# Fourier mixing and a gated convolution layer on one core: two matrix products per step in place of three, with work moved to ScalarE, VectorE and GpSimd

## Chip, cores and metric

The kernel runs on one core of one Trainium2 chip. The time is the device time in microseconds of one execution. A ratio is the mean time of one kernel's runs over that of the kernel before in the same rounds on the same chip, so it is not quite the ratio of the medians that are quoted beside it. "Faster" and "slower" mean by over 2%.

## The reference

```python
# x: (8, 3136, 256); w_in (256, 1024); conv_w (3, 1024); w_out (1024, 256), all float32
X = np.fft.fft(np.fft.fft(x, axis=1), axis=2).real      # mixing block
h = np.maximum(X @ w_in, 0.0)
conv_out = sum over k of conv_w[k] * (h shifted by k - 1 rows, zeros outside)
gate = 1.0 / (1.0 + np.exp(-conv_out))
out = (h * gate) @ w_out
```

## The kernel before

The mixing block is folded into `P` (cosines, even in the output row k) and `Q` (sines, odd in k; its last feature, the cosine feature D/2, is even). So columns k of `P` and `Q` give the rows k and S-k. The first layer works in **steps**: one batch, one chunk of columns (four per batch: 385, 386, 386 and 418 columns), one group of 128 features (eight per chunk); 256 steps in all, and 32 per batch. A step adds `G0 P + G1 Q` in a PSUM bank, takes the Relu (rows k), adds `G2 Q` with `G2 = -2 G1` in the same bank, and takes the Relu again (rows S-k, backwards). The rows of `h` are 769 to 833 columns wide. The second layer runs three steps behind.

```python
def front(s):                       # (cut)
    for i in range(2):
        mm(xs[s][:, 0:n], G[:, i, fs], PQ[b][i][:, ch.k0:ch.k1], i == 0, i == 1)
    act(h[:, ch.front], xs[s][:, 0:n], AF.Relu)

def back(s):                        # (cut)
    mm(xs[s][:, 0:n], G[:, 2, fs], PQ[b][1][:, ch.k0:ch.k1], False, True)
    act(hs[s][:, ch.back][:, ::-1], xs.pop(s)[:, ch.cols], AF.Relu)

def conv(s):                        # all three on VectorE
    ts(out=g, in0=h[:, 0:n], scalar1=cw[:, 0, f:f + 1], scalar2=None, op0=ALU.mult)
    for k in (1, 2):
        stt(out=g, in0=h[:, k:k + n], scalar=cw[:, k, f:f + 1], in1=g, op0=ALU.mult, op1=ALU.add)

def gate(s):
    act(g, g, AF.Sigmoid)
    vt(g, g, hs.pop(s)[:, 1:g.shape[1] + 1], op=ALU.mult)      # VectorE

# the order, step si; late: the second layer of step si - 3
front(si); late[:half]; back(si); late[half:]; conv(si); gate(si - 1); side work
```

Side work is the next batch's folds (VectorE, twelve operations per batch), its four DFT stages (16 matrix products each, then a copy on ScalarE and two sums on VectorE), and two such stages for the D/2 feature per pair of batches.

## Time and profile before

| | before |
|---|---|
| time, median of the first 3 runs | 1536.83 us (1535.79 to 1539.03) |
| TensorE busy | 1452.7 us, 95% |
| VectorE, ScalarE, GpSimd busy | 1143.9, 536.5, 68.5 us |
| an ordinary step, from the chain of waits | 4.53 us, TensorE without a gap |

The page has the busy time of each engine, its busy tenths in forty slices, the chain of work that ended last, and groups of instructions (line, engine, operation, output and inputs, shapes, count; then total busy us and mean ns; then the engine's idle time just before them and who ended it). The lines are in the prediction.

### The profile page before, as it was taken

The page shows a single profiled execution, that of the slowest core. Times are in us where ns is not written, and L with a number is a line of the kernel's source. Part 1 is how long each engine was busy: PE and PEld are TensorE (multiplying, and loading weights), DVE is VectorE, ACT ScalarE, POOL GpSimd, SP SyncE. Part 2 cuts the span into 40 slices and gives each one's busy share as a digit, 9 for nine tenths or more (in the row PEclk, how much of TensorE's full clock was granted, in tenths as well). Part 3 has the DMA queues.
Part 4 walks back from the last instruction along what each step waited for, and adds up shares of the span by engine and source line. Part 5 has one row for each costly group of instructions (what it writes and reads, how often), then busy time and mean ns, then how long its engine had stood idle before and what let it go on. Part 6 is the DMA issues. An engine that isn't in the chain of part 4 may idle for free.

```text
span 1535.6 us, 14574 instructions
## 1 busy us (share of the span) xinstructions
PE 1452.7 (95%) x5434; PEld 1003.6 (65%) x5434; DVE 1143.9 (74%) x1540; ACT 536.5 (35%) x1019; POOL 68.5 (4%) x81
## 2 busy tenths in 40 slices
PE   1758899999999999999999999999999999999998
PEld 0225556777767756677767756677766667677776
DVE  7699966689668966589767976679866666667775
ACT  0103323344334432344333433334423334334443
POOL 1201200001000100001000100000000000000000
PEclk9979999999999999999999999999999999999999
DMA  8501420013000220002200220000000000000001
GB/s 259 160 0 43 105 63 0 21 40 81 28 21 23 63 60 4 21 23 64 63 21 7 68 53 21 21 23 21 21 1 21 23 21 22 21 0 23 24 28 33
DMA packets 39014, 62.09 MB, mean 40 GB/s; under 512 B 5604, under 2 KB 30844, under 8 KB 38292
## 3 DMA queue, kind: packets, MB, share of 16 engines
q1 hardware_dynamic: 29084, 32.36, 6.4%
q0 software_dynamic: 8352, 24.21, 6.1%
q10 hardware_dynamic: 1508, 4.61, 1.0%
q8 instruction: 42, 0.69, 0.2%
q14 instruction: 28, 0.23, 0.1%
HBM read 35.41 MB, written 25.69 MB: 40 GB/s over the span
## 4 chain that ended last, share of the span: by engine, by line
PE 84%; DVE 10%; DMA 2%; ACT 2%; issue 1%; SPq 0%; ACTq 0%; DVEq 0%
PE pb L76 44%; PE po L76 41%; DMA out_dram<-os 2%; DVE g L364 2%; DVE xh L131 1%; DVE xh L124 1%; DVE g L369 1%; ACT os L388 1%; ACT g L368 1%; DVE g L362 1%; DMA raw<-in_moe_w_in_dram 1%; DVE w L141 0%; DVE nt L278 0%; DVE nt L266 0%; DVE nt L279 0%
## 5 line engine op out<-in xcount | busy, mean ns | idle before, releaser
L76 PE MATMUL po<-wout,g 128*128 128x256 f32 (+2 forms) x3200 | 773.4, 379 | 6.9 <-DVE g L369 6.7
L76 PEld LDWEIGHTS po<-wout,g 128*128 128x128 f32 (+2 forms) x3200 | 597.9, 187 | 216.2 <-issue 41.9
L364 DVE SCALAR_TENSOR_TENSOR g<-h,cw,g 128x770 f32<-128x770 f32 (+2 forms) x512 | 531.5, 1038 | 18.1
L76 PE MATMUL pb<-qt,G 128*128 128x386 f32 (+2 forms) x1024 | 426.4, 498 | 24.6 <-ACT h L346 17.2
L362 DVE TENSOR_SCALAR g<-h,cw 128x770 f32<-128x770 f32 (+2 forms) x256 | 161.3, 630 | 238.1 <-ACT h L354 233.3
L346 ACT ACTIVATE h<-pb 128x386 f32<-128x386 f32 (+2 forms) x256 | 127.9, 500 | 418.3 <-PE pb L76 393.3
L76 PEld LDWEIGHTS pb<-qt,G 128*128 128x128 f32 x1024 | 193.4, 190 | 118.8 <-ACT h L346 24.9
L369 DVE TENSOR_TENSOR g<-g,h 128x770 f32<-128x770 f32 (+2 forms) x256 | 248.8, 972 | 14.2 <-ACT g L368 14.2
L354 ACT ACTIVATE h<-pb 128x386 f32<-128x386 f32 (+2 forms) x256 | 127.9, 500 | 334.6 <-PE pb L76 334.6
L368 ACT ACTIVATE g<-g 128x770 f32<-128x770 f32 (+2 forms) x256 | 218.8, 855 | 22.8 <-DVE g L364 22.5
L76 PE MATMUL pb<-pt,G 128*128 128x386 f32 (+2 forms) x512 | 213.6, 499 | 3.0 <-DVE pt L174 3.0
L76 PE MATMUL pb<-tab,w 98*128 98x393 f32 (+7 forms) x512 | 173.7, 492 | 0.0
L76 PEld LDWEIGHTS pb<-tab,w 98*128 98x128 f32 (+3 forms) x512 | 96.5, 189 | 66.7 <-issue 0.7
L76 PEld LDWEIGHTS pb<-pt,G 128*128 128x128 f32 x512 | 97.0, 191 | 31.9 <-issue 5.9
L388 ACT COPY os<-po 128x256 f32<-128x256 f32 (+2 forms) x200 | 65.1, 375 | 53.0 <-DMA out_dram<-os 31.9
L76 PE MATMUL pb<-tab,ea 98*2 98x393 f32 (+7 forms) x160 | 56.3, 504 | 8.0 <-DVE ea L144 8.0
L171 ACT COPY as<-pb 128x393 f32<-128x393 f32 (+7 forms) x42 | 20.4, 485 | 120.3 <-PE pb L76 120.3
L76 PE MATMUL pb<-win,dm 128*128 128x512 f32 x24 | 15.7, 812 | 36.0 <-DVE nt L271 20.9
L93 POOL DMA_DIRECT2D xh<-in_x_dram x14 | 10.5, 752 | 822.6 <-DVE h L343 619.4
L76 PEld LDWEIGHTS pb<-tab,ea 98*2 98x2 f32 (+3 forms) x160 | 12.7, 85 | 47.7 <-issue 38.2
L98 POOL DMA_INDIRECT xh<-in_x_dram,idx x32 | 42.3, 1321 | 10.0 <-issue 9.7
L124 DVE TENSOR_TENSOR xh<-xh 99x1020 f32<-99x1020 f32 (+1 forms) x32 | 38.8, 1214 | 0.0
(46 smaller groups left out, 246.1 us busy)
## 6 DMA issues: line engine op xcount, KB each, us to landing
out_dram<-os SPq DMA_DIRECT2D x184, 128.0 KB
xh<-in_x_dram POOLq DMA_DIRECT2D x14, 784.0 KB, 6.6
tab<-dft_seq_dram SPq DMA_DIRECT2D x4, 1215.8 KB
raw<-in_moe_w_in_dram ACTq DMA_DIRECT2D x2, 1024.0 KB
raw<-in_moe_w_out_dram ACTq DMA_DIRECT2D x1, 2048.0 KB
xh<-in_x_dram SPq DMA_DIRECT2D x2, 784.0 KB
out_dram<-os SPq DMA_DIRECT2D x8, 127.0 KB
out_dram<-os SPq DMA_DIRECT2D x8, 65.0 KB
```

The costliest lines, as they stand in the source:

```text
L76: nc.tensor.matmul(o, l, r, start=start, stop=stop, skip_group_check=True)
L98: nc.gpsimd.indirect_dma_start(out=t[0:NP, 2 + s].rearrange("p q d -> p (q d)"), out_offset=None, in_=bass.AP(tensor=x.tensor, offset=x.of ...
L124: vt(a[:, :, 1:D], a[:, :, 1:D], r[:, :, D - 1:0:-1], op=ALU.add)
L131: vt(t[k, 3 - par], t[k, 0], t[k, 1], op=ALU.subtract if par else ALU.add)
L171: nc.scalar.copy(out=a, in_=ps[0])
L346: act(h[:, ch.front], xs[s][:, 0:n], AF.Relu)
L354: act(hs[s][:, ch.back][:, ::-1], xs.pop(s)[:, ch.cols], AF.Relu)
L362: ts(out=g, in0=h[:, 0:n], scalar1=cw[:, 0, f:f + 1], scalar2=None, op0=ALU.mult)
L364: stt(out=g, in0=h[:, k:k + n], scalar=cw[:, k, f:f + 1], in1=g, op0=ALU.mult, op1=ALU.add)
L368: act(g, g, AF.Sigmoid)
L369: vt(g, g, hs.pop(s)[:, 1:g.shape[1] + 1], op=ALU.mult)
L388: nc.scalar.copy(out=osb[0:m, j % 2], in_=pt[0:m, j % 2])
```

## The change

The intent is to take a product off TensorE, which bounds the kernel. `A = G0 P + (feature D/2)` is even in k and `B = G1 Q` is odd, so rows k are `Relu(A + B)` and rows S-k are `Relu(A - B)`: two products and two sums. The D/2 part of A is a rank-one term that ScalarE writes into the PSUM bank ahead of the product (the **seed**). The sums go to VectorE, and to make room there the first convolution product goes to ScalarE and the gate's multiplication to GpSimd. Feature group 3 keeps three products, and so does group 0 in the first chunk of a batch: 5 of 32 steps.

```diff
+def seed(s):
+    pa[s] = seeded()                                  # one of two banks of their own
+    act(pa[s][:, 0:n], eb[b][:, ch.k0:ch.k1], AF.Copy, scale=ge[:, f:f + 1])
+def products(s):                                      # where two(s); else as before
+    mm(xs[s][:, 0:n], G[0:P - 1, 1, fs], PQ[b][1][0:P - 1, ch.k0:ch.k1], True, True)
+    mm(pa[s][:, 0:n], G[:, 0, fs], PQ[b][0][:, ch.k0:ch.k1], False, True)
+def combine(s):
+    for i, (to, cols) in enumerate(open_h(s)):
+        act(nb[:, i, cols], p[:, cols], AF.Copy, scale=-1.0 if i else 1.0)
+        nc.vector._custom_dve(TENSOR_ADD_SAT, out=to, in0=a[:, cols], in1=nb[:, i, cols], s0=BIG, s1=0.0)
 def conv(s):
-    ts(out=g, in0=h[:, 0:n], scalar1=cw[:, 0, f:f + 1], scalar2=None, op0=ALU.mult)
+    act(g, h[:, 0:n], AF.Copy, scale=cw[:, 0, f:f + 1])
 def gate(s):
     act(g, g, AF.Sigmoid)
-    vt(g, g, hs.pop(s)[:, 1:g.shape[1] + 1], op=ALU.mult)
+    nc.gpsimd.tensor_tensor(g, g, hs.pop(s)[:, 1:g.shape[1] + 1], op=ALU.mult)
 # the order, step si (cut; before: front, late, back, late, conv, gate, side work)
+    products(si); combine(si); late; side work; conv(si); gate(si - 1); seed(si + 1)
 # (cut: PSUM pools 4 + 4 banks -> 2 + 2 + 4; the D/2 row spread over the partitions through
 #  DRAM once per batch; smaller G; buffers of the start shared)
```

More of the change, by code (lines that the diff above doesn't have):

```diff
@@ L6 @@
 from concourse._compat import with_exitstack
+from concourse.dve_ops import TENSOR_ADD_SAT
 from concourse.masks import make_identity
@@ L24 @@
 CUTS = (0, 384, 768, 1152)
+BIG = 3.4028234663852886e38
+THREE = (3,)
+FIRST = (0, 3)
 @with_exitstack
@@ L65 @@
     gp = ctx.enter_context(tc.tile_pool(name="gp", bufs=5))
+    nbp = ctx.enter_context(tc.tile_pool(name="nbp", bufs=2))
+    ebp = ctx.enter_context(tc.tile_pool(name="ebp", bufs=1))
     osp = ctx.enter_context(tc.tile_pool(name="osp", bufs=2))
-    psx = ctx.enter_context(tc.tile_pool(name="psx", bufs=4, space=PSUM))
+    psa = ctx.enter_context(tc.tile_pool(name="psa", bufs=2, space=PSUM))
+    psx = ctx.enter_context(tc.tile_pool(name="psx", bufs=2, space=PSUM))
     pso = ctx.enter_context(tc.tile_pool(name="pso", bufs=4, space=PSUM))
@@ L79, in bank, with seeded @@
         return psx.tile([P, 512], F32, name="pb", tag="pb")
+    def seeded():
+        return psa.tile([P, 512], F32, name="pa", tag="pa")
     xh = {}
@@ L157 @@
     et = {}
+    eb = {}
+    edp = ctx.enter_context(tc.tile_pool(name="edp", bufs=1, space=bass.MemoryType.DRAM))
+    ed = edp.tile([B, NK], F32, name="ed")
     def dft(st, lhs, m, lo_hi, even):
@@ L194, in f @@
                     nc.sync.dma_start(out=PQ[b][1][P - 1:P, :], in_=et[e][i:i + 1, :])
+                    nc.sync.dma_start(out=ed[b:b + 1, :], in_=et[e][i:i + 1, :])
                 dft(st, lambda k, q: wt[b][0:k, st, q, 0:m], m, outs(PQ[b][sn], m, par), sn == 0)
@@ L243 @@
     HW = max(c.w for c in chunks)
+    HN = max(c.k1 - c.k0 for c in chunks)
     PC = 512
@@ L295, in words @@
         return w if w.dtype == F32 else w.bitcast(I32)
-    ident = const.tile([3 * NF, 3 * NF], F32, name="ident")
+    ident = gp.tile([3 * NF, 3 * NF], F32, name="ident", tag="g")
     make_identity(nc, ident)
-    dm = const.tile([P, 2, 3, P], F32, name="dm")
-    cw24 = const.tile([3 * NF, 1, P], F32, name="cw24")
+    dm = gp.tile([P, 2, 3, P], F32, name="dm", tag="g")
+    cw24 = gp.tile([3 * NF, 1, P], F32, name="cw24", tag="g")
     wout = const.tile([P, NF, D], F32, name="wout")
@@ L316 @@
     late_w = load_weight(wout, words(moe_w_out).rearrange("(c p) o -> p c o", p=P), nc.vector, nc.scalar)
-    G = const.tile([P, 3, F], F32, name="G")
-    for g in range(3):
+    G = const.tile([P, 2, F], F32, name="G")
+    thirds = sorted(set(THREE + FIRST))
+    G2 = const.tile([P, len(thirds), P], F32, name="G2")
+    for i, m in enumerate(thirds):
+        p = bank()
+        for t in range(2):
+            mm(p[:, 0:P], dm[:, t, 2, :], win[t][:, 0, m * P:(m + 1) * P], t == 0, t == 1)
+        nc.scalar.copy(out=G2[:, i], in_=p[:, 0:P])
+    for g in range(2):
         for c in range(0, F, 512):
-            p = bank()
+            p = seeded() if g else bank()
             for t in range(2):
@@ L324 @@
             nc.scalar.copy(out=G[:, g, c:c + 512], in_=p)
+    ge = const.tile([P, NF], F32, name="ge")
+    p = bank()
+    for m in range(NF):
+        for t in range(2):
+            mm(p[:, m:m + 1], win[t][:, 0, m * P:(m + 1) * P], dm[:, t, 1, P - 1:P], t == 0, t == 1)
+    nc.scalar.copy(out=ge, in_=p[:, 0:NF])
     cw = const.tile([P, 3, NF], F32, name="cw")
@@ L331, with cut, two, spread @@
     rows = out.rearrange("b s d -> (b s) d")
-    hs, gs, xs, po = {}, {}, {}, {}
-    def front(s):
+    hs, gs, xs, pa, po = {}, {}, {}, {}, {}
+    def cut(s):
         b, c, f = s
         ch = chunks[c]
-        n = ch.k1 - ch.k0
-        fs = slice(f * P, (f + 1) * P)
-        xs[s] = bank()
+        return ch, ch.k1 - ch.k0, slice(f * P, (f + 1) * P)
+    def two(s):
+        return s[2] not in (THREE if s[1] else FIRST)
+    def spread(b):
+        e, i = EOF[b]
+        eb[b] = ebp.tile([P, NK], F32, name="eb", tag="eb")
+        nc.sync.dma_start(out=eb[b], in_=ed[b:b + 1, :].to_broadcast([P, NK]))
+    def seed(s):
+        b, c, f = s
+        ch, n, fs = cut(s)
+        pa[s] = seeded()
+        act(pa[s][:, 0:n], eb[b][:, ch.k0:ch.k1], AF.Copy, scale=ge[:, f:f + 1])
+    def products(s):
+        b, c, f = s
+        ch, n, fs = cut(s)
+        xs[s] = bank()
+        if two(s):
+            mm(xs[s][:, 0:n], G[0:P - 1, 1, fs], PQ[b][1][0:P - 1, ch.k0:ch.k1], True, True)
+            mm(pa[s][:, 0:n], G[:, 0, fs], PQ[b][0][:, ch.k0:ch.k1], False, True)
+        else:
+            for i in range(2):
+                mm(xs[s][:, 0:n], G[:, i, fs], PQ[b][i][:, ch.k0:ch.k1], i == 0, i == 1)
+    def third(s):
+        b, c, f = s
+        ch, n, fs = cut(s)
+        mm(xs[s][:, 0:n], G2[:, thirds.index(f)], PQ[b][1][:, ch.k0:ch.k1], False, True)
+    def open_h(s):
+        ch, n, fs = cut(s)
         h = hp.tile([P, HW], F32, name="h", tag="h")
@@ L343, in front @@
             nc.vector.memset(h[:, 0:ch.w:ch.w - 1], 0.0)
-        for i in range(2):
-            mm(xs[s][:, 0:n], G[:, i, fs], PQ[b][i][:, ch.k0:ch.k1], i == 0, i == 1)
-        act(h[:, ch.front], xs[s][:, 0:n], AF.Relu)
-    def back(s):
-        b, c, f = s
-        ch = chunks[c]
-        n = ch.k1 - ch.k0
-        fs = slice(f * P, (f + 1) * P)
-        mm(xs[s][:, 0:n], G[:, 2, fs], PQ[b][1][:, ch.k0:ch.k1], False, True)
-        act(hs[s][:, ch.back][:, ::-1], xs.pop(s)[:, ch.cols], AF.Relu)
+        return ((h[:, ch.front], slice(0, n)), (h[:, ch.back][:, ::-1], ch.cols))
+    def combine(s):
+        ch, n, fs = cut(s)
+        a, p = pa.pop(s), xs.pop(s)
+        nb = nbp.tile([P, 2, HN], F32, name="nb", tag="nb")
+        for i, (to, cols) in enumerate(open_h(s)):
+            act(nb[:, i, cols], p[:, cols], AF.Copy, scale=-1.0 if i else 1.0)
+            nc.vector._custom_dve(TENSOR_ADD_SAT, out=to, in0=a[:, cols], in1=nb[:, i, cols],
+                                  s0=BIG, s1=0.0)
     def conv(s):
@@ L417 @@
     for si in range(len(steps) + LAG):
+        s = steps[si] if si < len(steps) else None
         late = mm2_ops(steps[si - LAG]) if si >= LAG else []
-        cut = len(late) // 2
-        if si < len(steps):
-            front(steps[si])
-        for fn in late[:cut]:
-            fn()
-        if si < len(steps):
-            back(steps[si])
-        for fn in late[cut:]:
-            fn()
-        if si < len(steps):
-            conv(steps[si])
+        if s:
+            if si % per == 0:
+                spread(s[0])
+            if si == 0 and two(s):
+                seed(s)
+            products(s)
+            if two(s):
+                combine(s)
+            else:
+                (front, n), (back, cols) = open_h(s)
+                act(front, xs[s][:, n], AF.Relu)
+                for fn in late[:len(late) // 2]:
+                    fn()
+                late = late[len(late) // 2:]
+                third(s)
+                act(back, xs.pop(s)[:, cols], AF.Relu)
+        for fn in late:
+            fn()
+        for fn in side.get(si, []):
+            fn()
+        if s:
+            conv(s)
         if 0 <= si - 1 < len(steps):
             gate(steps[si - 1])
-        for fn in side.get(si, []):
-            fn()
+        if si + 1 < len(steps) and two(steps[si + 1]):
+            seed(steps[si + 1])
 _INS = ['x', 'moe_w_in', 'moe_conv_w', 'moe_w_out']
```

## The prediction

> **What bounds the kernel now.** I read four views. First the page's busy rows, slices and chain:
>
> ```profile
> PE 1452.7 (95%) x5434; PEld 1003.6 (65%) x5434; DVE 1143.9 (74%) x1540; ACT 536.5 (35%) x1019; POOL 68.5 (4%) x81
> ...
> PE   1758899999999999999999999999999999999998
> ...
> PEclk9979999999999999999999999999999999999999
> ...
> PE 84%; DVE 10%; DMA 2%; ACT 2%; issue 1%; SPq 0%; ACTq 0%; DVEq 0%
> ```
>
> TensorE is busy 95% of the span at full clock, and 84% of the chain that ended last is its work. Busy time of pipelined matmuls overlaps, so for the price of one product I took the chain in order of time, in a stretch with no side work (start, us, what; a float32 matmul shows as two records):
>
> ```profile
> 682.01 1.29 PE po L76 x6
> 683.30 1.29 PE pb L76 x4
> 684.60 1.29 PE po L76 x6
> 685.89 0.65 PE pb L76 x2
> 686.54 1.29 PE po L76 x6
> ```
>
> One step (one batch, chunk and feature group) repeats after 686.54 - 682.01 = 4.53 us with no gap: twelve records of the second layer (2.58 us for six output tiles) and three first-layer products of 0.65 us. The last chunk of a batch has 418 columns and seven tiles: the same view has 1.73 + 1.41 + 1.29 + 0.70 = 5.13 us. Where four records of first-layer products read 1.41, the stretches with a DFT product read 6.68 (at 611.72): a DFT stage adds 5.27 us. Third, the groups give the durations of what the change moves (mean ns after the comma):
>
> ```profile
> L364 DVE SCALAR_TENSOR_TENSOR g<-h,cw,g 128x770 f32<-128x770 f32 x256 | 261.5, 1021 | 9.0
> L369 DVE TENSOR_TENSOR g<-g,h 128x770 f32<-128x770 f32 x128 | 122.2, 955 | 3.2 <-ACT g L368 3.2
> L368 ACT ACTIVATE g<-g 128x770 f32<-128x770 f32 x128 | 107.7, 842 | 6.9 <-DVE g L364 6.7
> L362 DVE TENSOR_SCALAR g<-h,cw 128x770 f32<-128x770 f32 x128 | 79.5, 621 | 110.0 <-ACT h L354 110.0
> L354 ACT ACTIVATE h<-pb 128x386 f32<-128x386 f32 x128 | 63.2, 493 | 167.0 <-PE pb L76 167.0
> L388 ACT COPY os<-po 128x256 f32<-128x256 f32 x184 | 59.9, 375 | 47.8 <-DMA out_dram<-os 26.8 <-PE po L76 21.0
> L174 DVE TENSOR_TENSOR pt<-as,pb 128x392 f32<-128x392 f32 x8 | 4.5, 564 | 16.5 <-PE pb L76 16.5
> ```
>
> Fourth, who waits for whom: ScalarE waits for TensorE (393.3 and 334.6 us before its two Relus) and VectorE for ScalarE (233.3 us). TensorE's own waits in the steady part are near nothing: the others have slack.
>
> **What the Trainium skill says.** (1) "SBUF — State Buffer", Who interferes with whom: a VectorE instruction with two SBUF inputs contends with a GpSimd instruction that reads SBUF. The trace of before has no GpSimd arithmetic in the loop, so it neither agrees nor disagrees. (2) "GPSIMD Engine Reference", 3.1: a float32 [...]two-input operation of 2048 elements took 4497 ns there; scaled to 770 elements that is an estimate of 1.7 us for the gate's multiplication, against 0.955 measured on VectorE here. (3) "ScalarE: Activation LUTs", What ACT_TABLE_LOAD costs: 186 ns + 0.833 ns per element with immediates, about 93 ns more for a per-partition scale. For 770 elements that is 827 ns; the trace has 842, so it agrees, and I take 0.84 to 0.93 for the moved convolution product. (4) "PSUM — Partial Sum Buffer", The four PSUM rules: ScalarE writes do not change the bits that make a matmul accumulate. The seed therefore works only in banks where earlier matmuls set them, which the new pool's use while the weights are built arranges. This is about the result, not the time.
>
> **The change part by part.**
>
> *Removed from TensorE.* Feature group 3 keeps three products, and so does group 0 of the first chunk: 5 of 32 steps per batch, so 27 have two. Saved per batch: 20 x 0.647 + 7 x 0.705 = 17.9 us; times 8, **143 us**. If TensorE stayed as well fed as now the time would be 1537 - 143 = **1394 us**. That is the floor; a two-product step needs 4.53 - 0.65 = 3.88 us of TensorE. At the start fewer 512-column products are built but sixteen one-column ones are added; the DFT there waits for VectorE's folds in the trace (TensorE idle until 59.2 us), so I count 0.
>
> *VectorE.* Loses 161.3 us (first product, line 362) and 248.8 (gate's multiplication, line 369), gains 432 adds of about 0.56 us (taken from line 174, a sum of PSUM and SBUF of the same length) = 242: 1144 becomes about **976**. *ScalarE.* 432 Relus become 432 copies of equal cost; added are 216 seeds of about 0.53 us (114) and 256 convolution products of about 0.9 us (230): 536 becomes about **880**. *GpSimd.* 256 x 1.7 = **435** on top of 68. No total reaches TensorE's 1310 (1453 - 143).
>
> *The new order is tighter than the totals.* The built order shows that each seeded matmul waits for its seed, and ScalarE's order is: two copies, convolution product, the previous step's Sigmoid, then the next seed. So there is a loop from seed to seed: matmul to first add 0.85 us (in the trace a 386-column product starts at 701.92 and its Relu at 702.77), two adds 1.12, convolution product 0.75 (start to start, as ScalarE overlaps successive instructions), Sigmoid 0.73, seed 0.5, handovers 0.1: **4.05 us**, against 3.88 for TensorE. VectorE's own loop (two adds 1.12, wait for the product 0.84, two convolution terms of 1.02, gaps) is 4.05 too. Both are just over TensorE, without slack. What then costs, per batch:
> - ordinary two-product steps of the first three chunks, 20 x 0.17 = 3.4 us (the last chunk, 4.42 us of TensorE, has a little slack);
> - the step whose group-0 successor in the previous chunk's drain copies outputs: six copies and a wait for an output buffer put the convolution product some 2 us late; the third product in group 3, placed right behind it, needs no seed, but its Relu queues too: about 2 us x 4 = 8;
> - DFT steps: VectorE must do two sums after the DFT and then two convolution terms before the next add, 1.7 to 1.85 us late, 4 of them and one like it for the D/2 feature: about 8;
> - folds of the next batch between adds and convolution terms: 12 operations of 1.2 to 1.5 us of which 0.9 hides behind ScalarE's product: about 5.
>
> The sum is some 24 us per batch; with the last batch having no DFT, and the first a double set of folds, at most about **170 us** if every one is paid in full. That would give 1394 + 170 = 1564: nothing gained. They are not all paid in full: DFT steps fall on output-copy and three-product steps, and a backlog paid once is not paid again by the next wait. I choose a little over half, 96 us, and get **1490 us**. That share is my judgement, not a measurement.
>
> **The rivals.**
> (a) TensorE stays fed. For it: no other engine comes above about 75% busy. Against it: the loops of 4.05 us. Time 1395 to 1425.
> (b) The feed loop takes the whole gain: every late seed above counted in full. Time 1540 to 1590. The trace speaks for it by the durations; against it speaks that the third product kept in group 3 comes just behind the output copies, as though placed to absorb them.
> (c) GpSimd and VectorE fight for SBUF. The gate's multiplication becomes ready about 1.6 us after the convolution product began, while the first of VectorE's two-input terms runs, and there is a gap of some 0.04 us before the second. If GpSimd gets in there and shuts VectorE out, the second term comes 1.7 us later in each two-product step: up to 216 x 1.7 = 367 us, a time near 1800. Against it: in the next 2 us VectorE has adds with only one SBUF input, so GpSimd may fit there for nothing. A mild form (0.2 to 0.4 us a step) adds 40 to 90 us.
> (d) x loads are issued by GpSimd behind the multiplications: 3 to 5 us per half batch of its time. The three-step lag before the second layer gives over 3 us of slack, so below 15 us in all.
>
> **Range and chances.** (a) has about one chance in five, a part loss of 30 to 115 us about two in five, (b) about one in four, a harmful (c) about one in eight. So: predicted 1490 us, range 1410 to 1590, faster by over 2% (below 1506) 0.55, within 2% 0.27, slower 0.18.
>
> **What would show each step right or wrong.** TensorE's busy time should fall to about 1310 us, and its share below 90%, with waits of the seeded product on ScalarE's seed as its largest new wait. The chain should pass over seed, Sigmoid, convolution product and adds, instead of 84% TensorE. Adds should take 0.55 to 0.62 us, seeds 0.5 to 0.6, the moved convolution product 0.84 to 0.93, GpSimd's multiplication about 1.7. Convolution terms still at 1021 ns say there is no contention; longer ones, or idle time of VectorE between the two, say (c). The prediction is wrong upward if steps without side work last over 4.4 us, and downward if they last 3.9 and the chain stays TensorE's.

## The result and the profile after

The changed kernel is correct and took **1691.34 us** (median of 4 runs, 1690.9 to 1692.63) against 1537.21; the ratio is **1.1003**, 95% interval 1.0987 to 1.1018: slower by 10%. The page of the changed kernel (busy rows, TensorE's slices, the chain by engine):

```profile
PE 1373.3 (81%) x5034; PEld 919.6 (54%) x5034; DVE 1222.5 (72%) x1460; ACT 837.0 (50%) x1492; POOL 492.4 (29%) x337
...
PE   0957798877888798878888788887888888887877
...
DVE 42%; PE 24%; ACT 16%; issue 14%; DMA 3%; ACTq 0%; SPq 0%; POOLq 0%; DVEq 0%
```

TensorE is no longer the bound: 24% of the chain in place of 84%. VectorE leads the chain with 42%, but with 72% it is not full either, which is the mark of engines that wait in turn. VectorE's busy time is 1222 us where the prediction had 976. The groups of the changed kernel say where the difference is:

```profile
L427 DVE SCALAR_TENSOR_TENSOR g<-h,cw,g 128x770 f32<-128x770 f32 (+2 forms) x512 | 780.6, 1525 | 217.4 <-ACT g L425 208.4
L432 POOL TENSOR_TENSOR g<-g,h 128x770 f32<-128x770 f32 (+2 forms) x256 | 431.2, 1685 | 1122.2 <-ACT g L431 998.4
L425 ACT ACTIVATE g<-h,cw 128x770 f32<-128x770 f32 (+2 forms) x256 | 243.6, 952 | 416.9 <-DVE h L416 407.6
L83 PE MATMUL pa<-pt,G 128*128 128x386 f32 (+2 forms) x432 | 201.3, 548 | 225.7 <-ACT pa L383 225.7
L416 DVE CUSTOM_DVE_ANT_0 h<-pa,nb 128x386 f32<-128x386 f32 (+4 forms) x432 | 222.7, 555 | 1.5 <-PE pa L83 1.4
L383 ACT ACTIVATE pa<-eb,ge 128x386 f32<-128x386 f32 (+2 forms) x216 | 123.9, 574 | 0.0
```

The two convolution terms (L427) are the same instructions on the same shapes as before, where all 512 took 531.5 us; here they take 780.6. The moved and added work is about as long as predicted (adds 555 ns, seeds 574, ScalarE's product 952, GpSimd's multiplication 1685). TensorE idles 225.7 us before the seeded product, waiting for the seed. The stretches of the timeline of one ordinary step show both (start, us, engine, operation; in brackets the idle time before and what ended it):

```profile
763.23 0.94 ACT L425 ACTIVATE g<-h,cw 128x770 f32<-128x770 f32 x1 [2.31 <-DVE h L416]
...
764.07 0.83 ACT L431 ACTIVATE g<-g 128x769 f32<-128x769 f32 x1
764.20 3.24 DVE L427 SCALAR_TENSOR_TENSOR g<-h,cw,g 128x770 f32<-128x770 f32 x2 [1.06 <-ACT g L425]
764.81 0.57 ACT L383 ACTIVATE pa<-eb,ge 128x386 f32<-128x386 f32 x1
765.04 1.59 POOL L432 TENSOR_TENSOR g<-g,h 128x769 f32<-128x769 f32 x1 [1.44 <-PE pb L83]
...
765.43 0.92 PE L83 MATMUL pa<-pt,G 128*128 128x386 f32 x2 [1.08 <-ACT pa L383]
...
767.37 1.01 DVE L416 CUSTOM_DVE_ANT_0 h<-pa,nb 128x386 f32<-128x386 f32 x2
...
768.47 0.94 ACT L425 ACTIVATE g<-h,cw 128x770 f32<-128x770 f32 x1 [2.30 <-DVE h L416]
```

(GpSimd's line names "PE pb" as what ended its wait, but that product was long done; the Sigmoid of L431 ended at 764.90.) The step repeats after 768.47 - 763.23 = 5.24 us, where TensorE needs 3.88. The chain of waits splits VectorE's 3.24 us: 1.03 us for the first term, a gap of 0.03, then the second from 765.26 to 767.44. GpSimd's multiplication begins at 765.04, while the first term still runs, and ends at 766.63. From there to 767.44 are 0.81 us, most of a second term (1.02 us undisturbed). So the second term looks as though it stood still while GpSimd's instruction ran. The adds, and after them ScalarE's product, come later by that wait.

### The profile page after: what moved, and what is told of

The parts are those of the page before. It is cut to its first block, busy times and chain, and to the rows that moved or that the text cites. A ratio compares the mean times of both kernels' runs of the same rounds, so it can differ in the third digit from the quotient of the medians.

```text
span 1689.4 us, 15252 instructions
## 1 busy us (share of the span) xinstructions
PE 1373.3 (81%) x5034; PEld 919.6 (54%) x5034; DVE 1222.5 (72%) x1460; ACT 837.0 (50%) x1492; POOL 492.4 (29%) x337
## 4 chain that ended last, share of the span: by engine, by line
DVE 42%; PE 24%; ACT 16%; issue 14%; DMA 3%; ACTq 0%; SPq 0%; POOLq 0%; DVEq 0%
DVE g L427 22%; PE pb L83 13%; ACT g L425 10%; DVE h L416 9%; PE po L83 8%; PE pa L83 3%; DMA out_dram<-os 2%; ACT g L431 2%; ACT pa L383 2%; DVE xh L142 1%; DVE xh L135 1%; DVE w L152 1%; ACT os L451 1%; DVE w L151 1%; DVE qt L188 1%
## 5 line engine op out<-in xcount | busy, mean ns | idle before, releaser
L427 DVE SCALAR_TENSOR_TENSOR g<-h,cw,g 128x770 f32<-128x770 f32 (+2 forms) x512 | 780.6, 1525 | 217.4 <-ACT g L425 208.4
L432 POOL TENSOR_TENSOR g<-g,h 128x770 f32<-128x770 f32 (+2 forms) x256 | 431.2, 1685 | 1122.2 <-ACT g L431 998.4
L425 ACT ACTIVATE g<-h,cw 128x770 f32<-128x770 f32 (+2 forms) x256 | 243.6, 952 | 416.9 <-DVE h L416 407.6
L83 PE MATMUL pa<-pt,G 128*128 128x386 f32 (+2 forms) x432 | 201.3, 548 | 225.7 <-ACT pa L383 225.7
L83 PE MATMUL pb<-qt,G 127*128 127x386 f32 (+5 forms) x592 | 251.5, 506 | 38.8 <-ACT h L493 31.1
L83 PEld LDWEIGHTS pa<-pt,G 128*128 128x128 f32 x432 | 67.6, 190 | 352.7 <-ACT pa L383 345.8
L416 DVE CUSTOM_DVE_ANT_0 h<-pa,nb 128x386 f32<-128x386 f32 (+4 forms) x432 | 222.7, 555 | 1.5 <-PE pa L83 1.4
L431 ACT ACTIVATE g<-g 128x770 f32<-128x770 f32 (+2 forms) x256 | 216.1, 844 | 3.1 <-DVE g L427 3.1
L415 ACT ACTIVATE nb<-pb 128x386 f32<-128x386 f32 (+4 forms) x432 | 187.3, 483 | 25.5 <-PE pb L83 25.5
L83 PEld LDWEIGHTS pb<-qt,G 127*128 127x128 f32 (+1 forms) x592 | 111.3, 193 | 86.4 <-ACT h L493 41.9
L383 ACT ACTIVATE pa<-eb,ge 128x386 f32<-128x386 f32 (+2 forms) x216 | 123.9, 574 | 0.0
L188 DVE TENSOR_TENSOR qt<-as,pb 127x393 f32<-127x393 f32 (+1 forms) x16 | 9.0, 564 | 82.2 <-PE pb L83 41.6
```

The source lines that it names most:

```text
L83: nc.tensor.matmul(o, l, r, start=start, stop=stop, skip_group_check=True)
L188: vt(lo, a, ps[1], op=ALU.add)
L383: act(pa[s][:, 0:n], eb[b][:, ch.k0:ch.k1], AF.Copy, scale=ge[:, f:f + 1])
L415: act(nb[:, i, cols], p[:, cols], AF.Copy, scale=-1.0 if i else 1.0)
L416: nc.vector._custom_dve(TENSOR_ADD_SAT, out=to, in0=a[:, cols], in1=nb[:, i, cols], s0=BIG, s1=0.0)
L425: act(g, h[:, 0:n], AF.Copy, scale=cw[:, 0, f:f + 1])
```

## The experiments

Theory S: the second convolution term, which reads two tensors from SBUF, is shut out by GpSimd's multiplication, which reads SBUF too. The expectations call this "the port"; the runs show only which instruction waits for which. Theory L: the loop of waits from seed to seed costs the time and the contention does little. Five runs tell them apart; in all of them but the half dose, the kernel before took 1538.30 us.

**Gate's multiplication back on VectorE.**

```diff
-nc.gpsimd.tensor_tensor(g, g, hs.pop(s)[:, 1:g.shape[1] + 1], op=ALU.mult)
+vt(g, g, hs.pop(s)[:, 1:g.shape[1] + 1], op=ALU.mult)
```

> The changed kernel with the gate's multiplication back on VectorE, nothing else. Theory S ([...]GpSimd's multiplication shuts out VectorE's second convolution term): the convolution terms return from a mean of 1525 ns to about 1025 ns, but VectorE gets 0.955 us of multiplication per step instead of a 1.15 us wait, so a step goes from 5.24 to about 5.0 us and the time to about 1640 us (1600 to 1680). Theory L (the loop of waits alone, seed to adds to product to Sigmoid to seed, costs what was lost, contention matters little): VectorE has 245 us more to do in the same loop, the time rises to 1800 us or more.

Correct, 1667.57 us, ratio 1.0839. The convolution terms are back at their old length:

```profile
L427 DVE SCALAR_TENSOR_TENSOR g<-h,cw,g 128x770 f32<-128x770 f32 (+2 forms) x512 | 530.6, 1036 | 220.9 <-ACT g L425 211.8
```

VectorE does 248.6 us of multiplication more and the kernel is 24 us faster. This is S's figure and not L's (over 1800).

**GpSimd writes and does not read (wrong result).**

```diff
-nc.gpsimd.tensor_tensor(g, g, hs.pop(s)[:, 1:g.shape[1] + 1], op=ALU.mult)
+hs.pop(s)
+for _ in range(2):
+    nc.gpsimd.memset(g, 0.5)
```

> Wrong result on purpose: GpSimd fills the gate tile with a constant, twice, instead of multiplying; it has the same place in the order and the same waits but reads nothing from SBUF. Theory S: no contention[...], convolution terms at 1025 ns, steps of about 4.05 us, time 1420 to 1480 us. Theory L: convolution terms may change but the time stays over 1600 us.

1559.64 us, ratio 1.0139. The groups:

```profile
L427 DVE SCALAR_TENSOR_TENSOR g<-h,cw,g 128x770 f32<-128x770 f32 (+2 forms) x512 | 530.7, 1036 | 264.6 <-ACT g L425 255.6
L434 POOL MEMSET g<- 128x770 f32 (+2 forms) x512 | 386.3, 755 | 1030.2 <-ACT g L431 1015.4
```

GpSimd is busy for 1.5 us of each step in the same place, beside the same convolution terms, and these take 1036 ns. So it is GpSimd's reading, not its running, that holds them. The time falls by 132 us, but not to the 1420 to 1480 that S expected, and it went under L's 1600: **both theories have a part**. Without any contention 166 us remain over the floor of 1394. (The edit also frees `h` earlier, as nothing on GpSimd reads it, so 132 us is contention and whatever that gave.) An ordinary step takes 4.37 us here.

**A dose: GpSimd multiplies half the columns (wrong result).**

```diff
-nc.gpsimd.tensor_tensor(g, g, hs.pop(s)[:, 1:g.shape[1] + 1], op=ALU.mult)
+w = g.shape[1] // 2
+nc.gpsimd.tensor_tensor(g[:, 0:w], g[:, 0:w], hs.pop(s)[:, 1:w + 1], op=ALU.mult)
```

> Wrong result on purpose: the changed kernel, its order untouched, with GpSimd multiplying only the first half of the columns (0.8 in place of 1.6 us). A dose of the suspected cost: if VectorE's second term waits until GpSimd's instruction ends, the wait falls from 1.15 to about 0.4 us a step, the convolution terms from a mean of 1525 to about 1200 ns, and the time by 216 x 0.5 to 0.8 us to about 1570 to 1620 us (1691 with the whole, 1560 without any reading). If the cost were GpSimd's mere presence in the chain, it would not depend on the length.

1588.11 us, ratio 1.0314. The group, and one pair of convolution terms with the multiplication beside it in the timeline:

```profile
L427 DVE SCALAR_TENSOR_TENSOR g<-h,cw,g 128x770 f32<-128x770 f32 (+2 forms) x512 | 635.4, 1241 | 247.9 <-ACT g L425 238.8
```

```profile
764.48 2.56 DVE L427 SCALAR_TENSOR_TENSOR g<-h,cw,g 128x770 f32<-128x770 f32 x2 [1.07 <-ACT g L425]
765.25 0.97 POOL L433 TENSOR_TENSOR g<-g,h 128x385 f32<-128x385 f32 x1 [3.60 <-ACT g L431]
```

Both terms together take 2.56 us: 2.08 with GpSimd only writing, 3.24 with the whole multiplication. GpSimd ends at 766.22; the pair ends at 767.04, 0.82 us later, and with the whole multiplication it was 0.81: the wait ends with GpSimd's instruction, at both lengths. The three steps last 4.37 (writing only), 4.57 and 5.24 us. Time and convolution terms lie within what was expected.

**The kernel before with only the gate's multiplication moved to GpSimd.** The edit is that of `gate` in the change.

> The kernel before with the gate's multiplication moved to GpSimd and nothing else. Theory S: the convolution terms lengthen from a mean of 1038 ns to 1250 to 1550 ns here too, but VectorE has slack (0.62 + 2.06 + 1.2 = 3.9 us in a step of 4.53 us bound by TensorE), so the time stays within 2% of before, 1525 to 1560 us. If the lengthening comes from something else in the change (the new adds, ScalarE's product), the terms stay at 1038 ns.

Correct, 1569.97 us, ratio 1.0202 (interval 1.0172 to 1.0232): longer by about 2% (whether by more, the interval leaves open) and a little beyond the 1525 to 1560 us that S expected. The convolution terms take 1471 ns here too, with neither adds nor seeds. In the timeline even the first convolution product, a one-input instruction, is held:

```profile
705.12 1.54 POOL L369 TENSOR_TENSOR g<-g,h 128x769 f32<-128x769 f32 x1 [2.98 <-PE po L76]
705.27 1.81 DVE L362 TENSOR_SCALAR g<-h,cw 128x769 f32<-128x769 f32 x1
```

That product takes 0.62 us in the kernel before; here it ends at 707.08, 0.42 us after GpSimd. VectorE's slack in the step of 4.53 us hides most of the waits, not all: the convolution terms take 221 us more in all, and the time grows by 32 us.

**The next seed ahead of the previous step's Sigmoid.** The changed kernel with two statements exchanged.

```diff
-gate(si - 1); seed(si + 1)
+seed(si + 1); gate(si - 1)
```

> The changed kernel with ScalarE's next seed ahead of the previous step's Sigmoid, nothing else. The Sigmoid, and so GpSimd's multiplication, comes 0.5 to 0.6 us later, when VectorE's second convolution term should have started, and runs beside the adds, which have one SBUF input. Theory S: convolution terms at a mean of 1030 to 1150 ns, steps of 4.05 to 4.2 us, time 1420 to 1500 us. Theory L: only the seed comes 0.75 us sooner, and since VectorE's own loop is as long as before, the time falls by less than 50 us, to 1640 or more.

Correct, 1558.48 us, ratio 1.0124. It takes back 133 us without taking anything away, but is neither theory's figure. The timelines of VectorE and GpSimd show pairs of two kinds:

```profile
728.85 3.23 DVE L427 SCALAR_TENSOR_TENSOR g<-h,cw,g 128x770 f32<-128x770 f32 x2
729.72 1.55 POOL L432 TENSOR_TENSOR g<-g,h 128x770 f32<-128x770 f32 x1 [1.95 <-PE pb L83]
...
1303.38 2.08 DVE L427 SCALAR_TENSOR_TENSOR g<-h,cw,g 128x770 f32<-128x770 f32 x2 [1.07 <-ACT g L425]
1304.71 2.15 POOL L432 TENSOR_TENSOR g<-g,h 128x770 f32<-128x770 f32 x1 [1.94 <-ACT g L431]
```

Where GpSimd still comes before the second term, as at 729.72, the pair takes 3.23 us and GpSimd 1.55. Where it comes after the second term has begun, as at 1304.71, the pair takes 2.08 us and it is GpSimd that is held: 2.15 us, ending at 1306.86, which is 1.40 us after the pair. So each waits for the other, and here the one that came first was done first. The next pair starts at 1307.46, a step of 4.08 us. That is VectorE's own loop: two terms, two adds, and 1.07 us in which it waits for ScalarE's product.

The mean is 1236 ns, so less than half of the contention is left, about half of it in steps with folds. Taking all of the contention away gave 132 us, this order takes a good half of it away and gives 133; the rest of the gain is put down to the shorter seed loop, which no run shows alone.

What was left was taken as theory D (late seeds: at output copies, behind DFT stages, at folds) against theory C (the remaining contention sets it). All that follow start from this order.

**Output copies moved behind convolution product and seed.** Copies of a finished chunk are collected and issued after the seed.

```diff
-late (with its output copies); folds and DFT stages; conv(si); seed(si + 1); gate(si - 1)
+late; folds and DFT stages; conv(si); seed(si + 1); output copies; gate(si - 1)
```

> The kernel with the seed ahead of the Sigmoid (e3_seed_first, 1558 us), and the output copies of a finished chunk moved behind the convolution product and the seed on ScalarE. Theory D (what is left over the floor of 1394 us is a sum of late seeds: about 2 us at each of the 32 output drains, some 2 us after each of 36 DFT stages, the rest at folds): 1558 less 32 x 1.2 to 2 us = 1495 to 1520 us. Theory C (what is left is the port contention still in the trace, convolution terms at 1236 ns, and it sets the step): within 15 us of 1558.

Correct, 1607.49 us, ratio 1.046: 49 us **slower**, outside both expectations. The chain of waits shows why:

```profile
614.98 0.71 ACT os L454 x3
615.69 3.30 DMA out_dram<-os
...
619.74 0.74 ACT g L432
620.48 0.39 ACT h L497
...
620.92 1.28 PE pb L83 x2
```

Output buffers exist for four of the six tiles. Issued as one block behind the seed, the last two copies wait 3.03 us for the first tiles' DMA, and behind them in ScalarE's order stand the Sigmoid and the Relu that the third product waits for. In their old place the copies start as TensorE finishes each pair; no single wait for the DMA is over 1.8 us there, but their sum is about the same (41.6 us, here 40.6). There is a second part: after this wait TensorE ran slower for a while. The granted clock from 620 to 625 us is 0.66 (the two records at 620.92 take 1.28 us; the same product took 0.92 in the changed kernel, at 777.83), and from 345 us to 1600 it is 0.97, where the order before had 1.00: by estimate 0.03 x 1255 = 38 us of the 49. How the loss divides between the waits and the clock was not tested.

**DFT stages behind the convolution.** TensorE's order is unchanged; the stage's copy and sums come after the step's convolution terms in the other two engines' order.

```diff
-side work; conv(si); seed(si + 1); gate(si - 1)
+folds; conv(si); seed(si + 1); gate(si - 1); DFT stages
```

> e3_seed_first with the DFT stages issued behind the convolution on ScalarE and VectorE (TensorE's order is as it was), so that the two convolution terms no longer wait for the DFT. Theory D: 36 stages x 1 to 2 us sooner, 1490 to 1525 us. Theory C: within 15 us of 1558.

Correct, 1519.17 us, ratio 0.9879: 39 us less than with the seed moved alone (each against its own runs of before). The convolution terms stay at 1226 ns, so this gain is not contention: D holds for the DFT stages, at about 39 / 36 = 1.1 us each.

**Both, and the Sigmoid later still.** GpSimd's multiplication is to fall beside the adds.

```diff
-products(si); combine(si); late; folds; conv(si); seed(si + 1); gate(si - 1); DFT stages
+products(si); combine(si); gate(si - 2); late; folds; conv(si); seed(si + 1); output copies; DFT stages
```

> Both of these, and the Sigmoid of the step before moved behind the next step's two copies, one more step late, so that GpSimd's multiplication falls beside the adds. Theory D: both gains add and contention falls (convolution terms near 1100 ns): 1420 to 1480 us, faster than before. Theory C: contention goes too, so it also expects a gain, but the convolution terms must fall to 1100 ns for it; if they stay over 1200 and the time falls under 1490, C is wrong.

Correct, 1534.68 us, ratio 0.9989: 15 us slower than with the DFT stages moved alone, and D's 1420 to 1480 was missed. The convolution terms fell to 1137 ns. It holds the block of copies that was harmful above; that this eats the gain is likely and not shown here.

**Copies and DFT stages moved, and GpSimd only writing (wrong result).** The Sigmoid stays in its place behind the seed.

```diff
-late (with its output copies); folds; conv(si); seed(si + 1); gate(si - 1); DFT stages
+late; folds; conv(si); seed(si + 1); output copies; gate(si - 1), with memset; DFT stages
```

> Wrong result on purpose: seed first, output copies and DFT stages later, and GpSimd only fills a constant, so there is no contention at all. Theory D: all late seeds but those of the folds are gone: 1394 to 1440 us. If it stays over 1480, the loss is neither in the drains nor behind the DFT stages nor in the port.

1481.12 us, ratio 0.964. It missed D's 1440, and by the expectation's own mark (over 1480) the loss would lie neither in the output copies nor in the DFT stages nor in the port. The run can't say that, as it has the block of copies in it; without the block, the last run below comes to 1447. Its chain has stretches in which TensorE is the bound again:

```profile
744.20 0.65 PE pa L83 x2
744.86 2.59 PE po L83 x12
747.45 0.65 PE pb L83 x2
748.10 0.65 PE pa L83 x2
```

This is the step of two products, 748.10 - 744.20 = 3.90 us. The size of what the change removes is therefore as predicted (3.88).

**Small output buffers.** The DFT order, and four buffers of one tile in place of two of two tiles, in the same memory.

```diff
-osp = tc.tile_pool(name="osp", bufs=2)       # tiles of 2 x 256 columns
+osp = tc.tile_pool(name="osp", bufs=4)       # tiles of 256 columns
```

> e6_dft_later (1519 us) with four output buffers of one tile each in place of two of two tiles (same memory), so that ScalarE's last output copies wait less for the DMA of the first. In e6 ScalarE waited 42 us in all for it, in the middle of the order that the seeds hang on. Theory D: most of that comes back, 1485 to 1510 us. If the port contention hides it, 1510 to 1522 us.

Correct, **1507.74 us, ratio 0.9794** (interval 0.9777 to 0.981), near the upper end of D's span: the fastest correct version here, 11% less than the changed kernel takes. It is clearly faster than the kernel before, but whether by more than 2% the interval leaves open. ScalarE's wait for the output DMA fell from 42.0 to 22.3 us. The page and the convolution terms:

```profile
PE 1352.6 (90%) x5034; PEld 924.4 (61%) x5034; DVE 1084.8 (72%) x1460; ACT 846.9 (56%) x1492; POOL 580.0 (38%) x337
...
PE 59%; DVE 19%; ACT 9%; issue 8%; DMA 4%; POOL 1%; SPq 0%; ACTq 0%; DVEq 0%
...
L427 DVE SCALAR_TENSOR_TENSOR g<-h,cw,g 128x770 f32<-128x770 f32 (+2 forms) x512 | 631.9, 1234 | 278.2 <-ACT g L425 269.1
```

**The Sigmoid later on top of it.**

```diff
-combine(si); late; folds; conv(si); seed(si + 1); gate(si - 1); DFT stages
+combine(si); gate(si - 2); late; folds; conv(si); seed(si + 1); DFT stages
```

> e9 with the Sigmoid of a step moved behind the next step's two copies, so that GpSimd's multiplication falls beside the adds and the wait for the convolution product. Theory S: outside the fold steps VectorE's convolution terms are no longer held, their mean falls from 1236 ns (e3) towards 1100, and the time falls by 10 to 40 us below e9. If it is slower than e9, the later Sigmoid delays the second layer or the seed more than the port gives back.

Correct, 1508.76 us, ratio 0.9799: the same time, where S expected 10 to 40 us less. The convolution terms fell to 1159 ns, but the wait of the second layer's weight loads for GpSimd's result rose from 13.7 to 30.3 us, and the seeded product's wait from 59.5 to 67.5. That this is what used up the gain is likely and not shown.

**The version with small output buffers, GpSimd only writing (wrong result).** The edit to `gate` is that of the first run of this kind.

> Wrong result on purpose: e9 with GpSimd filling a constant instead of multiplying. It shows what the port still costs e9 and what the late seeds cost without it: 1410 to 1450 us if drains and DFT were the rest; the floor is 1394.

1446.84 us, ratio 0.9396; a few us inside the top of D's span. So contention still costs the best version up to 61 us. Of the 53 us that are left over the floor few are late seeds: the seeded products wait 5.9 us for them in all (59.5 with the multiplication). The ordinary steps still take 4.08 us, VectorE's own loop, where TensorE needs 3.88: by estimate 160 x 0.20 = 32 us.

| kernel | time, us | ratio | convolution terms, mean ns |
|---|---|---|---|
| before | 1537.21 | 1 | 1038 |
| changed | 1691.34 | 1.1003 | 1525 |
| gate on VectorE | 1667.57 | 1.0839 | 1036 |
| GpSimd writes only (wrong result) | 1559.64 | 1.0139 | 1036 |
| half the gate (wrong result) | 1588.11 | 1.0314 | 1241 |
| before, gate on GpSimd | 1569.97 | 1.0202 | 1471 |
| seed first | 1558.48 | 1.0124 | 1236 |
| seed first, DFT later, small output buffers | 1507.74 | 0.9794 | 1234 |
| seed first, DFT later, small output buffers, GpSimd writes only (wrong result) | 1446.84 | 0.9396 | 1038 |

## Why the prediction was wrong

It said 1490 us with 1590 as the upper end; 1691 was measured. Its sign for failing upward came (steps of 5.24 us, over 4.4), and so did its sign for rival (c) (convolution terms of 1525 ns). TensorE's busy time fell to 1373 us, not to 1310. By its own steps:

- **Bound before, and what is removed: right.** TensorE at its own pace does a two-product step in 3.90 us (3.88 predicted). The floor of 1394 us was never reached, but the version without contention came to 1447.
- **Costs of the moved work: nearly right.** Adds 555 ns (0.56 us), GpSimd 1685 (1.7 us; its shortest is 1542, so the mean is near in part because it holds waits for VectorE), ScalarE's product 952 (0.84 to 0.93), seeds 574 (0.53).
- **The loop from seed to seed, 4.05 us: too short.** Without contention a step takes 4.37 us. From the seeded product's start to the first add are 1.05 us, not 0.85; from product to Sigmoid 0.85, not 0.75; the rest is as predicted within 0.02. So the ordinary step lost 0.49 us against TensorE, not 0.17. VectorE's own loop, also put at 4.05, was right: it shows as 4.08 once the seed comes first.
- **"They are not all paid in full ... I choose a little over half, 96 us": this step failed.** The run in which GpSimd only writes is 166 us over the floor, where the sum had "at most about 170" (its own terms, 27 + 64 + 56 for seven batches with DFT + 35 for seven sets of folds, add to 182). So in total the waits were paid in full or nearly, but that the totals agree is partly luck. In that run the last batch, which has neither folds nor DFT stages, takes 147.0 us from its first convolution terms to those of its last step, against 145.7 in the kernel before, where 17.9 us were to be saved: it lost 19 us, about as much as the others (16 to 26). Ordinary steps alone make 20 x 0.49 = 10 us of that, not 3.4. A DFT stage, measured later, cost 1.1 us, not 1.7 to 1.85. There was no measurement behind the discount; both loops had been found longer than TensorE's step, so there was no slack to absorb a late seed.
- **Rival (c), given one chance in eight: this step failed too.** It names the mechanism that was found: GpSimd ready while the first term runs, in at the gap of about 0.03 us, the second term shut out until it is done. The argument against it ("GpSimd may fit there for nothing") fails because GpSimd does not wait for the adds: it is ready during the first term, and in the traces the instruction that came first went first (765.04 before 765.26 in the changed kernel, the other way round at 1304.71 in the run with the seed first). A lead of only 0.04 us did not help VectorE: in the kernel before with the gate on GpSimd, a term begun at 700.55 waited for a multiplication begun at 700.59. Only its size was off. It had 1.7 us a step; the second term waits 1.2, which makes VectorE's loop 4.08 + 1.16 = 5.24 us, and the step grows by 0.87, since without contention the loop from seed to seed holds it at 4.37. In all it is 132 us.

So the 297 us over the floor of 1394 are waits of 166 and contention of 132. That this adds up proves nothing, as both are differences to the same run. The split rests on that one run, in which GpSimd only writes, and on a floor that is worked out, not run. What makes up the part of the 53 us in the last run that is not VectorE's loop stays open.

## What to carry to other kernels

Before work is moved to GpSimd, ask which VectorE instructions run at that moment, and reckon that each of them that reads two tensors from SBUF and comes later waits until GpSimd's instruction ends (here 1.16 us for a GpSimd instruction of 1.59, and 0.48 for one of 0.97, at half the columns); order the queue so that GpSimd's instruction becomes ready after the last of them has started (then it waits itself, 2.15 us in place of 1.55). When a change ties TensorE to a result of the same step, add up the loop of waits first: totals of busy time (no engine over 81% here) say nothing about it, and a wait with no slack behind it is paid in full. Exchanging two statements brought back 133 of the 154 us lost, so the order is worth trying before the change is given up.

## What the Trainium skill lacked or had wrong

- "SBUF — State Buffer", Who interferes with whom: it says that a VectorE instruction with two SBUF inputs contends with a GpSimd one that reads SBUF, not with one that only writes, and the runs agree (1525 and 1036 ns). What it does not give is a row of dependent instructions: GpSimd, ready during one VectorE term, got in at a gap of 0.03 us before the next one, which depends on the first, and the next one then took 2.18 us instead of 1.02.
- The same section says that a VectorE instruction in a 2-port mode and GpSimd block each other fully. In the kernel before with the gate on GpSimd, the float32 one-input product took 1.81 us instead of 0.62: it agrees, if the product runs in such a mode, which the trace does not show.
- "GPSIMD Engine Reference", 3.1: its one size (4497 ns for an addition of 2048 elements) scales to an estimate of 1.69 us for 770; the undisturbed minimum of the multiplication was 1.54 and the median 1.60, which fits roughly. It gives no fixed part for GpSimd: 385 columns took 0.86 us at least, not half of 1.54. (The 0.97 us of the timeline above holds a wait for VectorE's first term.)
- "ScalarE: Activation LUTs", What ACT_TABLE_LOAD costs: about 93 ns for a per-partition scale; 938 ns against 842 for the Sigmoid of 770 columns in the kernel before, and 831 in the changed one, agrees roughly.
- No page says what a chain over three engines costs per round: five handovers with their instructions made 4.37 us, where the prediction, with 0.1 us for handovers, had 4.05; 0.20 of the difference lies between the seeded product's start and the first add.
